# Asking for the next piece of the token mix's weights at the end of the following step

## The chip, the core and the metric

The kernel runs on one core of one Trainium2 chip. The metric is the device time in microseconds (us). Each time stated for a kernel is the median of its runs. One execution of the kernel before was also profiled: that execution has a time of its own, and every row shown below comes from it.

The engines are called PE (matrix multiply), DVE (vector), ACT (scalar), POOL (GpSimd) and SP. SP computes nothing here: it issues nearly all DMAs, one after the other, in the order in which the program was written. A DMA that has to wait for a buffer holds every DMA behind it in SP's queue.

## The reference, cut to what matters

Three blocks follow one another: attention with a computed bias, a token mix with a channel mix, and a routed expert layer. Only the first and the weights of the second matter here.

```python
scores = scale * np.matmul(q, k.transpose(0, 1, 3, 2))          # q, k, v: (2, 8, 576, 64)
h = np.maximum(x @ w1 + b1, 0.0)                                # per pair of positions, 32 hidden
bias = h @ w2                                                   # (576, 576, 8)
scores = scores + bias.transpose(2, 0, 1)[None, :, :, :]
attn = np.exp(scores - np.max(scores, axis=-1, keepdims=True))  # then divided by its row sum
x = np.matmul(attn, v)
...
h = np.maximum(xt @ w_tok1, 0.0) @ w_tok2                       # token mix, 576 -> 256 -> 576
```

The token mix's weights w_tok1 (576 x 256) and w_tok2 (256 x 576) arrive as 64-bit floats. They are read during attention in nine pieces, each decoded to 32 bits on the chip.

## The kernel before, in words

Attention is a list of 40 steps, written out by hand: `for s in range(N + 2)`. The 576 query rows are cut into five row blocks (`its`: the 64 rows that are left over first, then four blocks of 128), and each block takes eight steps, one for each pair of heads of each batch. Step s computes the scores of its pair on PE (L359), adds the bias and takes the row minimum of the negated sum on DVE (L337), takes the exponential on ACT (L340), and does the transposes and the product with V for the steps just before it.

Beside these, steps 8 to 31 compute the bias of the row block to come, one group of 16 rows a step. `bias_hidden` makes the hidden units `hd` (L487 on ACT, L490 on DVE and POOL). `bias_mm` multiplies them on PE (L500), ACT copies the product out of PSUM into a tile `ev` (L503), and a DMA (L511) moves `ev` into 16 partitions of the block's bias tile. There are two `ev` buffers, so the copy of a group waits until the DMA of the group two steps before has landed. Eight groups make one bias tile, and the first scores of a new row block (steps 16, 24, 32) need all eight.

Within a step the order of work comes from `ORDER`. In "bias" (most steps from 8 on) `late` stands before `bias_mm`. In "edge" (steps 15, 23 and 31, the last of a row block) `bias_mm` stands second, before that step's scores, while `query_rest` stands near the end, with `late` behind it. Each order is also the order of SP's queue. `query_rest` runs in odd steps and issues four DMAs `qt<-qs` (L328). `load_q` runs at the top of even steps and issues `qn<-in_q_dram` (L245).

`late_step(s)` runs what the table `LATE` has for step s, among it `decode(p)` of a piece p, in steps 10, 12, 14, 16, 17, 20, 22, 24 and 26. `decode_f64` is one operation on ACT (L724) and three on DVE (L726, L728, L730), from the 64-bit tile `raw64` into 32 bits. `raw64` has two buffers (tag "kn"). Pieces 0 and 1 are fetched in step 8; every later `fetch` (L704) stands right behind the `decode` that frees its buffer. Pieces 0 to 3 are 256 KB each. Piece 4 is two DMAs of 128 KB. Pieces 5 to 8 are 288 KB each.

In the text, bias(13) means the DMA `bias<-ev` of step 13, ev(15) means ACT's copy L503 in step 15, and fetch 4 means the DMA or DMAs of piece 4.

Of the kernel before, what the change touches and what calls it, by code (L numbers as in the profile page):

```python
# [98 lines left out]
def body(ctx, tc, q, k, v, w1, b1, w2, wt1, wt2, wc1, wc2, wg, wl, mw1, mw2,  # L99
# [17 lines left out]
    with tc.manual_schedule():  # L117
        tok = ctx.enter_context(ExitStack())
        mix = TokenMix(nc, x)
        attention(tc, nc, tok, mix, q, k, v, w1, b1, w2, c_L, c_id, ident, x, wt1, wt2, prefill)  # L120
        if "x" in dbg:
            nc.sync.dma_start(dbg["x"], x)
        R = Routing(tc, nc, wg, wl, ident, c_tok, c_small, x2d, meta)
        X = Experts(tc, nc, R, Rings(tc, ctx, "big", side="right"), x_p, mw1, mw2, ident, x2d, meta, out)
        mixer(tc, nc, tok, mix, wc1, wc2, ident, x, R, X)
        if "x2" in dbg:
            nc.sync.dma_start(dbg["x2"], x2d)
        X.rest()
        X.close()
        R.close()  # L130


def attention(tc, nc, tok, mix, q, k, v, w1, b1, w2, c_L, c_id, ident, x, wt1, wt2, prefill):
# [10 lines left out]
    with ExitStack() as ctx:  # L144
# [65 lines left out]
        def load_k(i):  # L210

            b, pr = divmod(i, NP)
            n = nat_p.tile([128, 20, D], F32, name="kn", tag="kn", bufs=2)
            main, hs = n[:, 0:16].rearrange("p (n h) d -> p n h d", h=4), k[b, 2 * pr:2 * pr + 4]
            for j in range(NIT):
                nc.sync.dma_start(main[:, j], hs[:, 128 * j:128 * j + 128].rearrange("h p d -> p h d"))
            nc.sync.dma_start(n[0:64, 16:20], hs[:, 512:S].rearrange("h p d -> p h d"))
            for j in range(2):
                nat["k", i + j] = main[:, :, 2 * j:2 * j + 2], n[0:64, 16 + 2 * j:18 + 2 * j]

        def load_v(b):
            n = kv_p.tile([128, NIT + 1, H, D], F32, name=f"v{b}")


            nv, src = n.rearrange("p n (a e) d -> e p n a d", e=2), v[b].rearrange("(a e) p d -> e p a d", e=2)
            for e in range(2):
                r, z = (slice(64 * o, 64 * o + 64) for o in (e, 1 - e))
                nc.gpsimd.memset(nv[e][z, NIT], 0.0)
                for j in range(NIT):
                    nc.sync.dma_start(nv[e][:, j], src[e][64 * e + 128 * j:64 * e + 128 * j + 128])  # L230
                nc.sync.dma_start(nv[e][r, NIT], src[e][0:64] if e else src[e][512:S])
            nat["v", b] = n

        def load_q(it, i):

            b, pr = divmod(i, NP)
            n = nat_p.tile([128, 4, D], F32, name="qn", tag="qn", bufs=2)
            if it == NIT:
                tv = q[b, :, 512:S].rearrange("(a e) p d -> e p a d", e=2)
                for e in range(2):  # L240
                    nc.sync.dma_start(n[64 * e:64 * e + 64], tv[e])
                for j in range(NP):
                    nat["q", it, i + j] = n[:, j]
            else:
                nc.sync.dma_start(n, q[b, 2 * pr:2 * pr + 4, 128 * it:128 * it + 128].rearrange("h p d -> p h d"))  # L245
                nat["q", it, i] = n
# [268 lines left out]
        pieces = [(0, n) for n in range(5)] + [(1, n, a) for n in range(2) for a in range(2)]  # L515
        wt1_s = None

        def fetch(p):
            n = p[1]
            if p[0] == 0:  # L520
                src = wt1[128 * n:min(128 * n + 128, S)]
            else:
                src = wt2[128 * n:128 * n + 128, HALF * p[2]:HALF * p[2] + HALF]
            raws[p] = fetch_f64(nc, nat_p, src, "kn", 2, p[0] == 0 and n == 4)
# [65 lines left out]
        late = {}  # L590
# [13 lines left out]
        def late_step(s):  # L604
            for f, *a in late.get(s, ()):
                f(*a)
                if f is decode and pieces:
                    fetch(pieces.pop(0))

        load_const()  # L610
        bias_setup()
# [16 lines left out]
        for s in range(N + 2):  # L628

            bias = gi < len(groups) and s < N and s >= B * NP * (its.index(groups[gi] // 8) - 1)  # L630
            at = lambda d, n=N: steps[s + d] if 0 <= s + d < n else None
            two = lambda d: (s + d) % 2 == 0 and s + d >= B * NP and at(d)
            hide = groups[gi + 1] if bias and gi + 1 < len(groups) else None
            todo = {
                "late": (late_step, (s,)), "mix": (mixes[s][0], mixes[s][1:]) if s in mixes else (None, None),
                "tail_split": (tail_split, at(2, B * NP)), "tail_T": (tail_T, at(1, B * NP)),
                "query_T": (query_T, two(QO[0])), "query_split": (query_split, two(QO[1])), "query_rest": (query_rest, two(QO[2])),
                "key_split": (key_split, at(2, B * NP)),
                "normalize": (normalize, at(0)), "last_T": (last_T, at(-1)),
                "values": (values, at(-2)), "out_T": (out_T, at(-2)),  # L640
                "bias_mm": (bias_mm, (groups[gi],) if bias else None),
            }
            for j in range(4):
                todo[f"hidden{j}"] = bias_hidden, hide is not None and (hide, (j,))
                todo[f"key_T{j}"] = key_T, j < 2 and at(2, B * NP) and (*at(2), j)
                todo[f"scores{j}"] = scores, at(0) and (*at(0), j)
                todo[f"prob_T{j}"] = prob_T, at(-1) and (*at(-1), j)
            if two(QO[3]):
                load_q(*steps[s + QO[3]])
            for name in ORDER["edge" if bias and s % (B * NP) == B * NP - 1 else "first" if s < 3 else "mixed" if s < B * NP else "bias" if bias else "plain"]:  # L650
                f, a = todo[name]
                if a:
                    f(*(a[1:] if f in (key_split, key_T) else a))
            gi += bias
            if s == 1:
                load_k(6)
            if s == 2:
                load_v(1)
            if s == 10:
                prefill()  # L660
            if s == 8:
                for _ in range(2):
                    fetch(pieces.pop(0))
# [31 lines left out]
def fetch_f64(nc, pool, src, tag, bufs, twice=False):  # L695

    p = src.shape[0]
    wide = src.dtype != F32
    raw = pool.tile([128, *src.shape[1:], *([2] if wide else [])], I32 if wide else F32, name="raw64", tag=tag, bufs=bufs)
    if wide:  # L700
        e = "p k (n t) -> p k n t" if len(src.shape) == 3 else "p (n t) -> p n t"
        src = src.bitcast(I32).rearrange(e, t=2)
    for j in range(1 + twice):
        nc.sync.dma_start(raw[p * j:p * j + p], src)  # L704
    return raw, wide
# [1053 lines left out]
```

## Time and profile before

| | us |
|---|---|
| median of 3 runs | 587.43 (586.86 to 589.52) |
| the profiled execution's own time | 590.45 |
| its span, first to last instruction | 588.6 |
| PE busy | 546.4 (93% of the span) |
| DVE busy | 382.6 (65%) |
| ACT busy | 329.9 (56%) |
| POOL busy | 242.0 (41%) |
| mean granted TensorE clock | 0.978 of full speed |

Times in the rows count from the span's start. In a timeline row the first number is the start, the second the duration in us, and a bracket at the end gives how long the engine had been idle just before and what it waited for. Attention takes about the first 230 us. Steps 10 to 23, in which the change acts, lie between about 80 and 160 us.

### The profile page before, as it was taken

How to read it: one execution, taken by the hardware profiler on the slowest of the kernel's cores; microseconds unless marked ns; L12 is line 12 of the kernel's file. 1: busy time of each engine (PE TensorE's matmuls, PEld its weight loads, DVE VectorE, ACT ScalarE, POOL GpSimd, SP SyncE). 2: the span in 40 equal slices, each digit the busy share in tenths (PEclk: the TensorE clock that was granted, in tenths of full speed). 3: DMA queues.
4: the chain of work that ended last, by engine and by line, in shares of the span. 5: the costliest groups of instructions: out<-in, count | busy, mean ns of one | idle time of the engine just before them, and what ended most of it. 6: DMA issues, size and time to landing. Idle time of an engine off the chain costs nothing.

```text
span 588.6 us, 11960 instructions
## 1 busy us (share of the span) xinstructions
PE 546.4 (93%) x4306; PEld 431.8 (73%) x4306; DVE 382.6 (65%) x896; ACT 329.9 (56%) x608; POOL 242.0 (41%) x230
## 2 busy tenths in 40 slices
PE   8689699799899999998999999999999999999992
PEld 3356477577677797778999877787777778787871
DVE  6699588498797675598988644724374134668650
ACT  5578589489699685244444324221322257777760
POOL 4567466347566163034444400310004234666541
PEclk9899899799999999999999999999999999999997
DMA  7997989699777461044454010062001985566950
GB/s 160 133 171 130 150 158 157 84 170 167 118 132 134 87 167 52 0 143 117 141 155 164 4 69 21 1 245 96 37 18 21 359 306 179 152 225 240 369 187 12
DMA packets 72110, 79.90 MB, mean 136 GB/s; under 512 B 36822, under 2 KB 51420, under 8 KB 72044
## 3 DMA queue, kind: packets, MB, share of 16 engines
q1 hardware_dynamic: 67276, 73.72, 52.0%
q0 software_dynamic: 2176, 5.26, 2.7%
q8 instruction: 36, 0.59, 0.5%
q10 hardware_dynamic: 2592, 0.09, 0.3%
q14 instruction: 30, 0.25, 0.2%
HBM read 72.08 MB, written 5.34 MB: 132 GB/s over the span
## 4 chain that ended last, share of the span: by engine, by line
PE 62%; DVE 11%; DMA 11%; ACT 6%; issue 5%; SPq 2%; POOL 2%; ACTq 0%; POOLq 0%; DVEq 0%
PE ph L744 19%; PE po L744 15%; DMA bias<-ev 9%; PE py L744 5%; PE tp L425 4%; PE ps L500 4%; PE ps L359 3%; PE tp L410 3%; ACT t L340 2%; DVE t L337 2%; DVE K L272 1%; PE tp L744 1%; PE tp L1444 1%; DMA mt<-meta 1%; DMA raw<-in_moe_w_ch_dram 1%
## 5 line engine op out<-in xcount | busy, mean ns | idle before, releaser
L490 POOL TENSOR_SCALAR hd<-tabs,sc,negb 128x576 f32<-128x576 f32 x32 | 76.0, 2377 | 3.4 <-DMA qt<-qs 1.8
L340 ACT ACTIVATE t<-t,st 128x576 f32<-128x576 f32 x72 | 55.4, 771 | 27.4 <-DVE st L337 27.2
L337 DVE CUSTOM_DVE_ANT_0 t<-ps,bias 128x576 f32<-128x576 f32 x72 | 52.4, 751 | 23.1 <-DMA bias<-ev 13.1
L744 PE MATMUL po<-cw,h 128*128 128x512 f32 x272 | 67.3, 395 | 0.0
L359 PE MATMUL ps<-K,qt 128*128 128x288 f32 x320 | 56.3, 316 | 8.8 <-ACT ev L503 5.1
L744 PEld LDWEIGHTS po<-cw,h 128*128 128x128 f32 x272 | 49.8, 188 | 10.0 <-issue 0.4
L1407 DVE TENSOR_TENSOR big<-raw,big 128x1024 fp32r<-128x1024 f32 x30 | 42.6, 1441 | 22.2 <-ACT big L1406 22.1
L359 PEld LDWEIGHTS ps<-K,qt 128*128 128x128 f32 x320 | 46.4, 197 | 11.3 <-ACT ev L503 5.6
L500 PE MATMUL ps<-hd,wblk 128*32 128x288 f32 x576 | 44.1, 419 | 8.7 <-DVE st L337 6.3
L425 PE MATMUL tp<-pt,v 128*64 128x128 f32 (+1 forms) x800 | 49.8, 271 | 0.5 <-DVE K L272 0.5
L744 PE MATMUL py<-big,hT 128*128 128x512 f32 x184 | 47.8, 400 | 0.4 <-POOL big L1407 0.4
L1185 POOL DMA_INDIRECT meta<-tokid,posi x10 | 10.0, 998 | 90.9 <-DVE tokid L1182 55.0
L425 PEld LDWEIGHTS tp<-pt,v 128*64 128x64 f32 x800 | 40.7, 139 | 7.9 <-issue 5.2
L1406 ACT CAST big<-raw 128x1024 fp32r<-128x1024 f32 x44 | 44.2, 1055 | 2.8 <-DMA big<-in_moe_w_dram 1.0
L744 PE MATMUL ph<-big,xT 128*128 128x512 f32 x168 | 42.9, 403 | 0.0
L490 DVE TENSOR_SCALAR hd<-tabs,sc,negb 128x576 f32<-128x576 f32 x69 | 41.3, 630 | 0.2
L744 PEld LDWEIGHTS py<-big,hT 128*128 128x128 f32 x184 | 33.8, 188 | 8.6 <-POOL big L1407 0.8
L736 POOL TENSOR_TENSOR big<-wf,big 128x512 fp32r<-128x512 f32 x12 | 18.8, 1564 | 50.2 <-ACT big L735 50.2
L487 ACT ACTIVATE hd<-tabs,b1c,sc 128x576 f32<-128x576 f32 x43 | 36.9, 865 | 3.8 <-DVE sc L458 3.7
L1407 POOL TENSOR_TENSOR big<-raw,big 128x1024 fp32r<-128x1024 f32 x10 | 27.8, 2776 | 25.1 <-ACT big L1406 25.1
L503 ACT ACTIVATE ev<-ps,cb 128x576 f32<-128x576 f32 x36 | 26.6, 739 | 19.1 <-DMA bias<-ev 10.1
L744 PEld LDWEIGHTS ph<-big,xT 128*128 128x128 f32 x168 | 30.6, 189 | 8.6 <-issue 1.6
(302 smaller groups left out, 1196.2 us busy)
## 6 DMA issues: line engine op xcount, KB each, us to landing
raw<-in_moe_w_dram SPq DMA_DIRECT2D x48, 512.0 KB
raw<-in_moe_w_ch_dram SPq DMA_DIRECT2D x24, 512.0 KB
bias<-ev SPq DMA_DIRECT2D x32, 288.0 KB
qt<-qs SPq DMA_DIRECT2D x64, 128.0 KB
lw<-in_moe_w_dram SPq DMA_DIRECT2D x16, 512.0 KB
big<-in_moe_w_dram SPq DMA_DIRECT2D x8, 512.0 KB
lw<-in_moe_w_dram SPq DMA_DIRECT2D x16, 256.0 KB
big<-in_moe_w_dram SPq DMA_DIRECT2D x16, 256.0 KB
```

Source lines behind the costliest of these rows:

```text
L337: nc.vector.tensor_tensor_reduce(t.rearrange("p (a j) -> p a j", a=2), ps[:, :, 0:HALF], bs.rearrange("p (a j) -> p a j", a=2), op0=ALU.ad ...
L340: nc.scalar.activation(t, t, AF.Exp, bias=st[:, j:j + 1], scale=-1.0, accum_out=st[:, 2 + j:3 + j])
L359: nc.tensor.matmul(ps[:, hf, 0:HALF], lhsT=qt[:, j], rhs=K[k][:, hf * HALF:(hf + 1) * HALF], start=j == pairs[0][0], stop=j == pairs[-1][0])
L425: nc.tensor.matmul(po[64 * h:64 * h + 64, 0:rhs.shape[1]], lhsT=lhsT, rhs=rhs, start=j == 0, stop=j == 4)
L487: nc.scalar.activation(hd[:, qq], Lt[:, o:o + S], AF.Relu, bias=b1c, scale=sc[:, c])
L490: eng.tensor_scalar(hd[:, qq], Lt[:, o:o + S], sc[:, c], negb, ALU.mult, ALU.max)
L500: nc.tensor.matmul(ps[32 * qq:32 * qq + 32, hf, 0:HALF], lhsT=wblk, rhs=hd[:, qq, hf * HALF:(hf + 1) * HALF], start=True, stop=True)
L503: nc.scalar.activation(ev.rearrange("p (a b) -> p a b", a=2), ps[:, :, 0:HALF], AF.Identity, bias=cbs[hidden_by(g).replace("P", "V")])
L736: nc.gpsimd.tensor_tensor(lo, src, hi.bitcast(F32), ALU.subtract)
L744: nc.tensor.matmul(out, lhsT=lhs[a], rhs=rhs[b], start=first and i == 0, stop=last and i == 2)
L1406: nc.scalar.copy(hi, raw)
L1407: (nc.gpsimd if c == 3 and t else nc.vector).tensor_tensor(lo, raw, hi.bitcast(F32), ALU.subtract)
```

## The change

The fetch no longer stands behind its `decode`. Instead a new function, called at the end of step s, issues one fetch if step s - 1 had a `decode`. The seven fetches that stood in steps 10, 12, 14, 16, 17, 20 and 22 now stand at the ends of steps 11, 13, 15, 17, 18, 21 and 23. The pieces, their order, the buffers and the decodes stay as they were.

```diff
         def late_step(s):
             for f, *a in late.get(s, ()):
                 f(*a)
-                if f is decode and pieces:
-                    fetch(pieces.pop(0))
+
+        def late_fetch(s):
+
+            if pieces and any(f is decode for f, *_ in late.get(s, ())):
+                fetch(pieces.pop(0))
 
         load_const()
         bias_setup()
@@ -652,6 +655,7 @@
                 if a:
                     f(*(a[1:] if f in (key_split, key_T) else a))
             gi += bias
+            late_fetch(s - 1)
             if s == 1:
                 load_k(6)
             if s == 2:
```

## Rows read from the trace of the kernel before

**Rows 1.** The page, part 2: busy share of the DMA engines in 40 slices of 14.7 us.
```profile
DMA  7997989699777461044454010062001985566950
```

**Rows 2.** Who waited for whom, 75 to 200 us: total, times, longest.
```profile
ACT ev L503 <- DMA bias<-ev: 5.7, 2, 5.0
...
DVE t L337 <- DMA bias<-ev: 3.8, 2, 2.0
```

**Rows 3.** The timeline of PE, steps 15, 23 and the start of 24.
```profile
104.86 0.77 PE L359 MATMUL ps<-K,qt 128*128 128x288 f32 x4
109.85 1.33 PE L359 MATMUL ps<-K,qt 128*128 128x288 f32 x4 [4.22 <-ACT ev L503]
...
149.23 1.18 PE L500 MATMUL ps<-hd,wblk 128*32 128x288 f32 x16
...
152.53 0.80 PE L359 MATMUL ps<-K,qt 128*128 128x288 f32 x4 [0.89 <-ACT ev L503]
...
159.56 0.69 PE L500 MATMUL ps<-hd,wblk 128*32 128x288 f32 x8 [1.66 <-DVE st L337]
```

**Rows 4.** The timeline of ACT: copies to ev (L503) and decodes (L724).
```profile
101.73 0.45 ACT L724 ACTIVATE wt_s<-raw 128x256 f32<-128x256 f32 x1
...
109.06 0.74 ACT L503 ACTIVATE ev<-ps,cb 128x576 f32<-128x576 f32 x1 [5.03 <-DMA bias<-ev]
...
123.92 0.43 ACT L724 ACTIVATE wt_s<-raw 128x256 f32<-128x256 f32 x1
...
151.73 0.74 ACT L503 ACTIVATE ev<-ps,cb 128x576 f32<-128x576 f32 x1 [2.24 <-PE ps L359]
...
192.25 0.74 ACT L503 ACTIVATE ev<-ps,cb 128x576 f32<-128x576 f32 x1 [1.04 <-PE ps L500]
```

**Rows 5.** The chain that ended last: start, us from issue to landing.
```profile
90.35 7.43 DMA bias<-ev
...
99.20 9.76 DMA bias<-ev
...
152.50 6.08 DMA bias<-ev
...
193.02 5.03 DMA bias<-ev
```

**Rows 6.** Stretches: length, five engines' busy us, PEclk, DMA share, GB/s.
```profile
85.00:110.00 25.00, 20.78 (x240) 15.49 (x239) 19.12 (x59) 17.74 (x36) 13.97 (x8) 0.99 1.04 147
...
96.00:97.00 1.00, 1.00 (x20) 0.59 (x20) 1.00 (x5) 1.00 (x3) 1.00 (x1) 1.00 1.00 277
...
122.00:123.00 1.00, 1.00 (x22) 0.83 (x22) 1.00 (x5) 1.00 (x2) 1.00 (x2) 1.00 0.79 286
...
156.00:157.00 1.00, 1.00 (x14) 0.81 (x14) 0.69 (x2) 1.00 (x2) 0.92 (x2) 1.00 0.43 45
```

**Rows 7.** The same view and columns, around the fall of PE's clock.
```profile
109.00:110.00 1.00, 0.15 (x1) 0.15 (x1) 0.00 (x0) 0.94 (x2) 0.00 (x0) 0.65 0.47 49
...
115.00:116.00 1.00, 1.00 (x6) 1.00 (x6) 0.29 (x1) 0.98 (x2) 0.91 (x2) 0.50 0.00 0
116.00:117.00 1.00, 1.00 (x10) 0.81 (x11) 0.81 (x3) 0.37 (x1) 1.00 (x2) 0.93 0.00 0
```

**Rows 8.** The timeline of SP: fetches (L704) and the qt DMAs of step 15.
```profile
94.07 0.33 SPq L704 DMA_DIRECT2D raw<-in_moe_w_tok_dram  x1
...
104.06 1.16 SPq L704 DMA_DIRECT2D raw<-in_moe_w_tok_dram  x2
...
116.08 2.67 SPq L328 DMA_DIRECT2D qt<-qs  x4
...
120.64 0.35 SPq L704 DMA_DIRECT2D raw<-in_moe_w_tok_dram  x1
...
150.19 0.35 SPq L704 DMA_DIRECT2D raw<-in_moe_w_tok_dram  x1
```

**Rows 9.** The timeline of DVE, first scores of row block two (step 16).
```profile
116.19 0.76 DVE L337 CUSTOM_DVE_ANT_0 t<-ps,bias 128x576 f32<-128x576 f32 x1 [0.67 <-PE ps L359]
```

## The prediction, made before the changed kernel was run

> **What bounds the kernel now.** I read the page's slices first, for the stretch in which the change acts. The DMA engines are nine tenths busy or close to it in most of the first ten slices [rows 1], which is attention up to 147 us. So the change moves traffic inside a stretch where the DMA engines have little left; elsewhere such a move would hardly show.
>
> Then the waits between 75 and 200 us, to see who suffers [rows 2]. Two kinds matter: ACT's copy to `ev` waits for a bias DMA to land (5.7 us in two waits, one of them 5.0), and the softmax on DVE waits for one (3.8 us in two).
>
> Then PE's own timeline, because only what PE loses reaches the end. From 85 to 110 us PE is busy 20.78 of 25 us [rows 6], and the 4.22 us left are one hole, in step 15 before 109.85 [rows 3]. Around step 23 there are two more, 0.89 us before 152.53 and 1.66 us before 159.56. These three, 6.77 us together, are all that this change can win back, with what PE loses to a half clock behind the first hole. That hole is worth following: PE waits for ev(15), which starts at 109.06 after 5.03 us of idle ACT [rows 4], and which waited for bias(13), issued at 99.20 and landed 9.76 us later [rows 5]. Bias DMAs took 7.43 us from 90.35, 6.08 from 152.50 and 5.03 from 193.02; the last is from step 31, where no fetch is near. So a bias DMA costs some 5 us at best, and the rest is traffic ahead of it or beside it.
>
> **The change, part by part.** It adds no instruction and no byte. Seven fetches move by one to two steps, past these entries of SP's queue: the bias DMA of the step of the decode, what the next step puts there (`load_q` if it is even, the four `qt` DMAs if it is odd), and that next step's bias DMA. None of the passed entries now stands behind a wait for the decode's last DVE operation. New waits: none on SP, since the buffer has long been free.
>
> Even-step bias DMAs are issued earlier. That alone is worth nothing: the two `ev` waits sum to 5.7 us, the long one is step 15's, so 0.6 us is all that ACT ever waited for one of them, and PE had no hole there [rows 2, 3]. The two `ev` buffers are the cover.
>
> *Term a, step 15.* Fetch 3, asked for at 94.07 [rows 8], stands ahead of bias(13); after, it stands behind. The DMA engines are continuously busy in that stretch (share 1.04 [rows 6]), so what leaves the queue ahead shortens the landing by its service time. A fetch shows as a burst: 277 GB/s in 96 to 97 us [rows 6]; 256 KB at that rate is 0.95 us. Fetch 2 is ahead of bias(13) before and after, fetch 4 behind in both. So bias(13) lands at about 108.0 instead of 108.96 and PE resumes at 108.9.
>
> The clock takes a part of it. PE stopped at 105.63; its granted clock fell from 2.4 to 1.2 GHz at 109.3 (mean 0.65 over 109 to 110) and came back at 116.07 (0.93 over 116 to 117) [rows 3, 7]. If it still falls there, the 0.95 us gained are 0.4 at full and 0.55 at half speed, worth **0.68 us**. Bounds: nothing, if a fetch behind a bias DMA slows it as much as one ahead; the whole hole of 4.22 us and half of the 6.22 us from 109.85 to 116.07, if the stall ends.
>
> *Term b, ev(23).* It starts at 151.73, and the row names PE's L359, but the copy reads nothing of that. Its own product, L500, ended at 150.41 (149.23 + 1.18). In step 31, without a fetch nearby, ev(31) is released by L500 itself [rows 3, 4]. So I read the extra 1.3 us as the landing of bias(21), two steps back, and fetch 7 moves from ahead of bias(21) to behind it: 0.95 us again. PE's hole there is 0.89 us, so **0.89 us**. Bounds: 0 and 0.89.
>
> *Term c, bias(23).* Fetch 8, issued at 150.19, goes from ahead of bias(22) and bias(23) to behind the `qt` DMAs of step 23 [rows 8]. Bias(23) should then land like bias(31): 5.03 us instead of 6.08, **1.05 us** off the hole of 1.66 [rows 3, 5]. Bounds: 0 and 1.66.
>
> *Term d, the piece that is now late.* Six of the seven pieces keep time to spare. The shortest of them is piece 2, asked for behind bias(11) at 91 us and read by ACT at 101.73, 10.7 us later [rows 4, 5], longer than the slowest bias landing. Piece 4 is different. Step 15 has `query_rest` near its end, so fetch 4 moves from 104.06 to behind the four `qt` DMAs, which end at 118.75, and its two DMAs take 1.16 us of issue; ACT reads it at 123.92 [rows 4, 8]. Second half issued at 119.35. A fetch asked for at 120.64 had its burst in 122 to 123 us [rows 6, 8], about 2.4 us from issue to the last byte. Landing follows the data by about 2.2 us (bias(23) faded at 156.4, share 0.43 over 156 to 157, and landed at 158.58 [rows 5, 6]). That makes 4.6 us and 123.95: just too late or just in time. I take **+0.2 us**, by the nearest row. Bounds: 0, since earlier data gain nothing, and 2.9 us, if it takes the 7.43 us of a loaded bias DMA [rows 5]. ACT runs in order, so a late piece holds ev(17) and the exponentials of step 18.
>
> The Trainium skill (Trainium Kernel Development and Optimization, Best Practices) tells to double-buffer and overlap DMA with compute, which speaks against asking later; here the piece's time in hand before 123.92 falls from 19.9 to 5.2 us [rows 4, 8], and by that rule term d would be at its upper bound, 2.9 us, and the sum +0.3 us.
>
> *Sum.* -0.68 - 0.89 - 1.05 + 0.2 = **-2.4 us**. Against the profiled execution's own 590.45 (span 588.6 and 1.85 around it) that is 588.0. That execution stands 3.0 us above the median of the runs, with the same holes, so I take the sum off the median: 587.43 - 2.4 = **585.0 us**, 0.41% faster. Behind step 24 the rest follows attention's end and shifts as a whole, I assume.
>
> **The rivals.**
>
> *R1, the half clock goes too.* If PE resumes earlier or the fall comes at another moment, PE's work from 109.85 to 116.07 runs at full speed. Worth at most 3.1 us, but the first softmax of step 16, at 116.19 [rows 9], needs bias(15), issued when ev(15) ends (109.8) and landing no sooner than 5.03 us later, 114.8; so 1.35 us. Total -0.95 - 1.35 - 0.89 - 1.05 + 0.2 = -4.0: 583.4 us. For it: 3.3 us of idleness remain instead of 4.22. Against it: the clock fell 3.7 us after PE stopped, not far above what remains [rows 3, 7]. Chance 0.15.
>
> *R2, a fetch behind costs what it cost ahead.* Bias(13) took 4.7 us more than bias(31), far more than one burst of 0.95. If the DMAs behind share the engines with it, fetch 3, now right behind, slows it as before, and fetch 7 does so to bias(21): terms a and b are gone, c and d stay, -0.85: 586.6 us. Chance 0.22. The Trainium skill (DMA: Bandwidth & Descriptors, Queues, rings and completion order) says that one engine starts descriptors in order, but a later one may finish its write first; that permits this rival and does not price it. No row before shows which holds.
>
> *R3, slower.* Fetch 4 lands late. Its place is the decode in step 17, on ACT at 123.92. With the loaded 7.43 us it is 2.9 us late; ACT stops, DVE's L728 and PE follow, and a hole like step 15's would cost half a clock again, 3.1 us [rows 3, 7]. 2.9 + 3.1 - 2.6 (terms a to c) = +3.4: 590.8 us. Without the clock it turns slower than before once the piece is 2.6 us late. Against it: the DMA engines moved nothing from 115 to 117 us [rows 7], so the queue is short there. Chance 0.08.
>
> *R4, it does nothing that shows.* The fetches certainly move, as SP's queue is in order, but the bias DMAs may be bound by their own writes into 16 partitions: 587.4 us. Chance 0.10. The forecast keeps 0.45.
>
> **How the numbers follow.** About 0.5% (2.9 us) is what a measurement of this kernel can tell from no change. Faster by more than that: nearly all of R1 (0.14) and a third of the forecast's case, where a or c come out larger (0.16): 0.30. Slower by more: R3 and a little scatter: 0.08. The rest 0.62. The range goes from 582.2, below R1 by the scatter of the runs shown, to 588.5, above R4 by the same; R3 and a complete end of the stall lie outside.
>
> **What would show it.** In the changed trace: fetches right behind bias(11), bias(13) and bias(21), and behind the `qt` DMAs of steps 15 and 23; bias(13) landing in about 8.8 us, ACT's wait before ev(15) near 4.1 us and PE's hole near 3.3, with a half clock after it; ev(23) released by L500; bias(23) landing in 5.0 us and the 1.66 us hole down to 0.6; less than 0.5 us of idle ACT before step 17's L724. It is wrong if the landing of bias(13) does not change (R2), if no half clock follows step 15 (R1), or if ACT waits for piece 4 by more than 2 us (R3).

## The result, and the profile after

The changed kernel takes 584.0 us (median of 20 runs, 581.57 to 587.8) against 588.91 us for the kernel before (20 runs, 586.36 to 592.03). The ratio is 0.991, with a 95% interval of 0.9891 to 0.9929: 0.9% faster. The forecast was 0.41%.

The page of the changed kernel: the span and PE's busy time, then the granted clock and the DMA engines' busy share in 40 slices.

```profile
span 582.3 us, 11959 instructions
## 1 busy us (share of the span) xinstructions
PE 545.5 (94%) x4306; PEld 430.3 (74%) x4306; DVE 383.9 (66%) x896; ACT 329.5 (57%) x608; POOL 242.1 (42%) x230
...
PEclk8979889999999999999999999999999999999997
DMA  6997988698697351143443020081002985566950
```

PE's busy time hardly moved (545.5 us against 546.4); idle time went. Of the waits between 75 and 200 us [rows 2], ACT's for a bias DMA is gone from the list, and DVE's fell from 3.8 to 1.8 us:

```profile
ACT ev L503 <- PE ps L500: 4.8, 7, 1.0
...
DVE t L337 <- DMA bias<-ev: 1.8, 1, 1.8
```

PE's timeline, every idle stretch that it lists from 75 to 160 us. The holes of 4.22, 0.89 and 1.66 us [rows 3], and one of 0.33 not shown there, became four that sum to 2.67 us:

```profile
112.25 1.18 PE L500 MATMUL ps<-hd,wblk 128*32 128x288 f32 x16 [0.64 <-DVE st L337]
122.75 1.18 PE L500 MATMUL ps<-hd,wblk 128*32 128x288 f32 x16 [0.48 <-DVE st L337]
152.64 1.18 PE L500 MATMUL ps<-hd,wblk 128*32 128x288 f32 x16 [1.09 <-DVE st L337]
156.69 0.33 PE L397 MATMUL tp<-ident,t 128*128 128x128 f32 x1 [0.46 <-DVE x L448]
```

The stretches of [rows 6] (length, busy us of PE, PEld, DVE, ACT and POOL, granted clock, DMA share, GB/s). PE is busy throughout 85 to 110 us, and no half clock follows; before, the clock fell to 0.5 there [rows 7]:

```profile
85.00:110.00 25.00, 25.00 (x286) 19.60 (x284) 21.90 (x67) 22.32 (x46) 14.68 (x9) 1.00 0.85 154
110.00:117.00 7.00, 6.36 (x73) 4.87 (x74) 5.82 (x18) 5.15 (x11) 3.71 (x3) 1.00 0.56 137
```

ACT's timeline, with ev(15), the decode of piece 4 and ev(23), the counterparts of [rows 4]. Both copies to `ev` are released by their own product L500; the decode has no idle time before it:

```profile
105.39 0.74 ACT L503 ACTIVATE ev<-ps,cb 128x576 f32<-128x576 f32 x1 [1.04 <-PE ps L500]
...
118.76 0.42 ACT L728 ACTIVATE wt_s<-raw 128x256 f32<-128x256 f32 x1
...
145.33 0.74 ACT L503 ACTIVATE ev<-ps,cb 128x576 f32<-128x576 f32 x1 [1.04 <-PE ps L500]
```

SP's timeline around step 15, the counterpart of [rows 8]:

```profile
99.51 0.58 SPq L511 DMA_DIRECT2D bias<-ev  x1
100.19 0.54 SPq L708 DMA_DIRECT2D raw<-in_moe_w_tok_dram  x1
100.78 0.43 SPq L245 DMA_DIRECT2D qn<-in_q_dram  x1
103.86 2.84 SPq L511 DMA_DIRECT2D bias<-ev  x2
110.84 2.63 SPq L328 DMA_DIRECT2D qt<-qs  x4
113.57 1.20 SPq L708 DMA_DIRECT2D raw<-in_moe_w_tok_dram  x2
```

Bias(13), issued at 99.51, had landed when ev(15) started at 105.39: at most 5.9 us instead of 9.76 [rows 5]. Bias(14) goes out at 103.86, right when ev(14) ends (103.10 + 0.74); before, it waited behind fetch 4 until 105.3.

### The profile page after: what moved, and what is told of

Its sections match the earlier page's. It is cut to its first block, busy times and chain, and to the rows that moved or that the text cites. A ratio compares the mean times of both kernels' runs of the same rounds, so it can differ in the third digit from the quotient of the medians.

```text
span 582.3 us, 11959 instructions
## 1 busy us (share of the span) xinstructions
PE 545.5 (94%) x4306; PEld 430.3 (74%) x4306; DVE 383.9 (66%) x896; ACT 329.5 (57%) x608; POOL 242.1 (42%) x230
## 4 chain that ended last, share of the span: by engine, by line
PE 65%; DVE 12%; DMA 7%; issue 5%; ACT 5%; SPq 2%; POOL 2%; ACTq 0%; POOLq 0%; DVEq 0%
PE ph L748 20%; PE po L748 16%; DMA bias<-ev 6%; PE py L748 5%; PE ps L500 5%; PE tp L425 4%; PE ps L359 3%; PE tp L410 3%; DVE t L337 2%; ACT t L340 2%; PE tp L748 1%; DVE K L272 1%; DMA mt<-meta 1%; PE tp L1448 1%; DVE raw L732 1%
## 5 line engine op out<-in xcount | busy, mean ns | idle before, releaser
L359 PE MATMUL ps<-K,qt 128*128 128x288 f32 x320 | 54.0, 309 | 4.4 <-DVE qt L199 3.5
L500 PE MATMUL ps<-hd,wblk 128*32 128x288 f32 x576 | 47.7, 440 | 7.5 <-DVE st L337 6.5
L359 PEld LDWEIGHTS ps<-K,qt 128*128 128x128 f32 x320 | 45.0, 192 | 6.7 <-DVE qt L199 2.3
L500 PEld LDWEIGHTS ps<-hd,wblk 128*32 128x32 f32 x576 | 17.2, 115 | 24.1 <-DVE st L337 7.9
```

The source lines that it names most:

```text
L359: nc.tensor.matmul(ps[:, hf, 0:HALF], lhsT=qt[:, j], rhs=K[k][:, hf * HALF:(hf + 1) * HALF], start=j == pairs[0][0], stop=j == pairs[-1][0])
L500: nc.tensor.matmul(ps[32 * qq:32 * qq + 32, hf, 0:HALF], lhsT=wblk, rhs=hd[:, qq, hf * HALF:(hf + 1) * HALF], start=True, stop=True)
```

## The experiments

Two theories after this: the *hold* (SP stood at the fetch until the decode's last DVE operation, and the even-step bias DMA behind it went out late) and the *traffic* (the fetch's bytes lay ahead of the bias DMAs). Ratios are to the kernel before, run beside each.

**third_buffer.** Fetch in its old place in the program, but no wait:

```diff
-            raws[p] = fetch_f64(nc, nat_p, src, "kn", 2, p[0] == 0 and n == 4)
+            i = order.index(p)
+            tag, bufs = ("raw3", 1) if i % 3 == 2 else ("kn", 2)
+            raws[p] = fetch_f64(nc, nat_p, src, tag, bufs, p[0] == 0 and n == 4)
```

> The kernel before, with a third buffer for the pieces: each fetch stays where it was, ahead of the bias DMA of the decode's step, but no longer waits for the decode, so it holds nothing. Theory H (the hold: what cost the time was SP standing at the fetch until the decode's last DVE operation, which issued the even-step bias DMAs 1.0 to 1.8 us late): the gain of the changed kernel is there, 0.7 to 1.0% under the kernel before, and PE's hole before ev(15) is under 1 us. Theory T (the traffic: 256 KB ahead of each pair of bias DMAs): as the kernel before within 0.2%, hole about 4.2 us and the half clock behind it.

583.77 us, ratio 0.9925 (0.9898 to 0.9953): nearly the whole gain, by the hold theory. Its SP and ACT timelines:

```profile
99.89 0.58 SPq L511 DMA_DIRECT2D bias<-ev  x1
100.52 0.59 SPq L245 DMA_DIRECT2D qn<-in_q_dram  x1
101.20 1.18 SPq L707 DMA_DIRECT2D raw<-in_moe_w_tok_dram  x2
104.26 2.88 SPq L511 DMA_DIRECT2D bias<-ev  x2
```
```profile
105.78 0.74 ACT L503 ACTIVATE ev<-ps,cb 128x576 f32<-128x576 f32 x1 [1.04 <-PE ps L500]
```

The order in the queue is that of the kernel before: fetch 4, then bias(14) and bias(15). But SP, which waits for nothing, asks for the fetch at 101.20, 3 us before bias(14) at 104.26; in the kernel before these were 104.06 and 105.32, 1.3 us apart. So the order alone does not make the cost; when the issues come matters too.

**hold_only** and **no_hold.** The changed kernel with a 1 KB DMA in the seven old places; in the first it reads the decode's result, in the control the identity matrix:

```diff
+        scratch = scr_p.tile([16, 16], F32, name="scratch")
...
                 f(*a)
+                if f is decode and s < 24:
+                    p = a[0]
+                    done = raws[p] if p[0] else wt1_s[:, p[1]]
+                    nc.sync.dma_start(scratch[0:16], done[0:16, 0:16])
```

> The changed kernel, with a 1 KB DMA in each of the seven old places that reads the decode's result, so SP waits there for the decode as before, while the fetch and its bytes stay in the new place. Adds seven issues of about 0.4 us. H: the time of the kernel before within 0.3%, hole of 3 to 5 us before ev(15). T: the time of the changed kernel, 0.7 to 1.0% under the kernel before.

> The control of the run with the added wait: the same seven 1 KB DMAs in the same places, reading the identity matrix, which is there from the start, so SP waits for nothing. Both theories: the time of the changed kernel within 0.2%, no hole before ev(15). If it is slower, the added issues cost by themselves and the other run must be read against this one.

With the hold 586.11 us, 0.996 (0.994 to 0.9979); the control 584.27 us, 0.9919 (0.9893 to 0.9945). So the waits cost 1.84 us (586.11 - 584.27, medians of 12 and 6 runs), with no byte of a fetch moved. That is less than half of what the hold theory alone had asked for, and more than the traffic theory had. SP's timeline with the hold, step 14; ACT's at ev(15) with the hold; PE's at step 16 with the hold; and PE's at the same place in the control:

```profile
105.57 0.33 SPq L612 DMA_DIRECT2D scratch<-wt_s  x1
106.00 2.24 SPq L512 DMA_DIRECT2D bias<-ev  x2
```
```profile
106.50 0.74 ACT L504 ACTIVATE ev<-ps,cb 128x576 f32<-128x576 f32 x1 [1.48 <-DMA bias<-ev]
```
```profile
114.35 1.18 PE L501 MATMUL ps<-hd,wblk 128*32 128x288 f32 x16 [1.68 <-DVE st L338]
```
```profile
113.72 1.18 PE L501 MATMUL ps<-hd,wblk 128*32 128x288 f32 x16 [0.79 <-DVE st L338]
```

With the hold ev(15) waits 1.48 us for bias(13), which stands behind a held bias(12); in the control ev(15) is released by its own product. The hold also puts bias(14) 1.3 us before bias(15) instead of 2.3 (issued at 106.00 and 107.27 here, at 105.19 and 107.48 in the control), and the first scores of the next row block wait for both.

**same_step.** The fetch at the end of the decode's own step: no hold, but its bytes ahead of the next step's `qt` and bias DMAs.

```diff
-            late_fetch(s - 1)
+            late_fetch(s)
```

> The fetch at the end of the step of its decode: behind that step's bias DMA, but still ahead of the next step's qt DMAs and of the odd-step bias DMA that ev(15), ev(23) and the next row block wait for. H: all of the gain, 0.7 to 1.0%, since no bias DMA stands behind the wait. T: little of it, under 0.3%, hole before ev(15) of 3 us or more, since bias(13) and bias(23) still have the bytes ahead.

585.99 us, 0.9961 (0.9938 to 0.9984): less than half the gain, and 1.72 us above the control no_hold, so bytes in this place count too. Bias(13) took 6.71 us (the chain that ended last), and ACT waited for it:

```profile
99.12 6.71 DMA bias<-ev
```
```profile
105.93 0.74 ACT L503 ACTIVATE ev<-ps,cb 128x576 f32<-128x576 f32 x1 [1.95 <-DMA bias<-ev]
```

**behind_qt.** One place earlier than the change: behind the `qt` DMAs, straight ahead of the odd-step bias DMA.

```diff
+                if name == "query_rest":
+                    late_fetch(s - 1)
             gi += bias
-            late_fetch(s - 1)
```

> The changed kernel with each fetch one place earlier: behind the qt DMAs and ahead of the odd-step bias DMA. SP waits for nothing there. If only the hold costs, as the changed kernel within 0.2% and no wait of ev(15). If the bytes straight ahead of bias(13) count too, that DMA lands 1 to 2 us later, ev(15) waits 0.5 to 2 us for it, and the time is 0.2 to 0.4% above the changed kernel.

584.36 us, 0.9938 (0.9907 to 0.997). The interval doesn't tell it from the change. The profiled execution, at 585.91 us, has the mechanism: ACT waited for bias(13), which took 7.57 us.

```profile
108.20 0.74 ACT L503 ACTIVATE ev<-ps,cb 128x576 f32<-128x576 f32 x1 [3.90 <-DMA bias<-ev]
```

**first_three** and **last_four.** The change for the decodes of steps 10 to 14 alone, or of steps 16 to 22 alone (the other fetches stay behind their `decode`). The diff is that of first_three; last_four has `s < 15` and `s > 15` in the two places:

```diff
+                if f is decode and pieces and s > 15:
+                    fetch(pieces.pop(0))
...
-            if pieces and any(f is decode for f, *_ in late.get(s, ())):
+            if pieces and s < 15 and any(f is decode for f, *_ in late.get(s, ())):
```

> Only the fetches of steps 10, 12 and 14 are moved; those of steps 16 to 22 stand where they stood before. If the gain is mostly the stall of step 15 (4.2 us of hole and up to 3.1 us of half clock), this has most of it: 0.6 to 0.8% under the kernel before. If steps 15 and 23 count alike, as the prediction's terms had it (0.7 against 1.9 us), about a quarter: 0.1 to 0.3%.

> Only the fetches of steps 16, 17, 20 and 22 are moved. First case: the stall of step 15 is there as before, 0.1 to 0.3% under the kernel before, hole before the first scores of step 24 about 1 us smaller. By the prediction's terms b and c: 0.3% (1.9 us).

585.92 us, 0.996 (0.9937 to 0.9984), and 586.64 us, 0.997 (0.9949 to 0.9991): 2.4 and 1.7 us off 588.33. They add up to 4.1 of the 4.9 us. In first_three step 15 has no stall, but another came, in step 19, behind the unmoved fetches of steps 16 and 17: the chain's bias DMA, then ACT's wait.

```profile
120.98 10.78 DMA bias<-ev
```
```profile
131.87 0.74 ACT L503 ACTIVATE ev<-ps,cb 128x576 f32<-128x576 f32 x1 [3.50 <-DMA bias<-ev]
```

In last_four, whose program up to step 15 is that of the kernel before, ACT's timeline has a shorter wait for bias(13) than the 5.03 us of [rows 4], and no half clock followed. PE's timeline has the larger hole one step later, before step 16's L500:

```profile
105.82 0.74 ACT L503 ACTIVATE ev<-ps,cb 128x576 f32<-128x576 f32 x1 [2.03 <-DMA bias<-ev]
```
```profile
106.61 0.80 PE L359 MATMUL ps<-K,qt 128*128 128x288 f32 x4 [0.68 <-ACT ev L503]
...
114.38 1.18 PE L500 MATMUL ps<-hd,wblk 128*32 128x288 f32 x16 [2.39 <-DVE st L337]
```

The changed kernel has only 0.64 us of these 3.07. So the stall's size and place vary between executions; the profiled one before, 1.5 us above the median of 20, had a large one.

**hold_edges** and **hold_others.** The 1 KB DMA that waits, in steps 14 and 22 only, or in the five other steps only (`if f is decode and s in (14, 22)`, `s in (10, 12, 16, 17, 20)`).

> The changed kernel with the 1 KB DMA that waits for the decode in steps 14 and 22 only, the even steps just before the edge steps 15 and 23. Theory E (the hold costs at the edges: it issues bias(14) and bias(22) so late that bias(15) and bias(23), which the next row block waits for, land behind them): nearly all of the cost of the seven holds is here, 585.5 to 586.5 us, 0.35 to 0.45% under the kernel before. Theory S (each hold adds to the backlog in the queue): a third of that cost or less, under 585.0 us, at least 0.6% under.

> The changed kernel with the 1 KB DMA that waits for the decode in steps 10, 12, 16, 17 and 20 only. E: as without any hold, 583.8 to 584.8 us, 0.6 to 0.9% under the kernel before. S: two thirds of the cost or more, 585.3 us or above, at most 0.5% under.

587.64 us, 0.997 (0.9952 to 0.9989), and 585.81 us, 0.9936 (0.9915 to 0.9957). Neither theory fits. In the ratios the two edge steps cost 0.6% over the change's 0.991, clear of its interval, and more than theory E had asked for. The other five cost 0.26%, which the intervals don't tell from nothing; nor do they tell whether the two costs add up to that of the seven in hold_only (0.5%). The profiled executions show late DMAs in both. With holds at the edges alone bias(15) took 6.38 us; with the others alone bias(13) was late, as in hold_only:

```profile
105.89 6.38 DMA bias<-ev
```
```profile
106.13 0.74 ACT L504 ACTIVATE ev<-ps,cb 128x576 f32<-128x576 f32 x1 [1.48 <-DMA bias<-ev]
```

**twice.** A second 256 KB into an unread tile behind each moved fetch:

```diff
-                fetch(pieces.pop(0))
+                p = pieces.pop(0)
+                fetch(p)
+                fetch_f64(nc, nat_p, wt1[128 * (s % 4):128 * (s % 4) + 128], "spare", 1)
```

> The changed kernel with a second fetch of 256 KB, into a tile that nothing reads, behind each moved fetch: 1.8 MB more in the same stretch, all in the new places. Leaves nothing out. If the new place is one that nothing waits behind, within 0.2% of the changed kernel. If the DMA engines have no room left in the stretch (the share is 0.82 to 0.85 of 85 to 110 us without it), the stall before ev(15) is back and the time is 0.5% or more above the changed kernel.

588.46 us, 0.9987 (0.9965 to 1.001): the whole gain is gone. So the stretch has no room for 1.8 MB more, even in the new places. But ev(15) did not wait for a DMA; the largest hole came one step later, at the first scores of step 16 (PE's timeline), with a half clock behind it. What the softmax there waited for, the trace does not name. The stretch moved 169 GB/s at a share of 0.93, more than the kernel before at 1.04.

```profile
115.42 1.18 PE L500 MATMUL ps<-hd,wblk 128*32 128x288 f32 x16 [2.05 <-DVE st L337]
```
```profile
85.00:110.00 25.00, 25.00 (x295) 19.05 (x283) 22.30 (x68) 22.32 (x46) 14.02 (x8) 1.00 0.93 169
```

**dma_alone.** The computation is left out. Only the DMAs of a step pair run, in 14 groups; each group is issued, then DVE reads each landing (the inner loop, cut):

```python
for group in ("b", "t", "f", "n", "bb", "bt", "bn", "fb", "ft", "tb", "btbn", "fbtbn", "btbfn", "bftbn"):
    for _ in range(3):
        for r in [what[w]() for w in group]:
            r()
        ...
```

> Leaves the whole computation out and writes zeros: only the DMAs of one step pair, issued from SP in 14 groups, three times each, with DVE reading each landing. Measures bias (b), the four qt (t), a 256 KB fetch (f) and qn (n), alone and one behind the other: b, t, f, n, bb, bt, bn, fb, ft, tb, btbn, fbtbn, btbfn, bftbn. If the engines simply serve in order, a group takes the sum of its members' data times: fbtbn is 1 us longer than btbn, and the second b lands 1 us later. If transfers that overlap slow each other, b behind or beside t takes more than its time alone, and a fetch ahead of btbn costs the second b more than 1 us, one behind it nothing.

A letter is one DMA: b a bias DMA, t a `qt` DMA, f a fetch, n a `qn` DMA. One repeat each of btbn, fbtbn, btbfn and bftbn, first SP's issue of the group's first DMA, then DVE's read of its second bias DMA:

```profile
188.57 0.59 SPq L122 DMA_DIRECT2D bias<-ev  x1
...
210.75 0.35 SPq L132 DMA_DIRECT2D raw<-in_moe_w_tok_dram  x1
...
245.21 0.60 SPq L122 DMA_DIRECT2D bias<-ev  x1
...
278.03 0.59 SPq L122 DMA_DIRECT2D bias<-ev  x1
```
```profile
198.09 0.14 DVE L123 COPY seen<-bias 16x1 f32<-16x1 f32 x1 [3.48 <-DMA bias<-ev]
...
221.86 0.14 DVE L123 COPY seen<-bias 16x1 f32<-16x1 f32 x1 [3.85 <-DMA bias<-ev]
...
254.68 0.14 DVE L123 COPY seen<-bias 16x1 f32<-16x1 f32 x1 [3.43 <-DMA bias<-ev]
...
288.24 0.14 DVE L123 COPY seen<-bias 16x1 f32<-16x1 f32 x1 [3.54 <-DMA bias<-ev]
```

From first issue to the read: 9.52 us without a fetch, 11.11 with one ahead, 9.47 with one behind the second bias DMA, 10.21 with one behind the first. The other repeats with one ahead gave 11.30 and 10.48. These times hold SP's own work for the extra issue, 0.4 us when the fetch goes first (210.75 to 211.15) and 0.7 between. Counted from its own issue, the first bias DMA is read after 5.4 to 5.95 us with a fetch ahead, against 4.9 without: 0.5 to 1.1 us for the bytes. With a fetch between, the second bias DMA is read 6.2 us after its own issue, as without a fetch. So with nothing else running, bytes ahead cost a bias DMA about what term a assumed, and bytes behind nothing.

**spread.** An attempt to beat both: later decodes, so that most fetches leave the crowded stretch.

```diff
-... decode=[10, 12, 14, 16, 17, 20, 22, 24, 26], split_wt2=[-3, -4, 0, -4, 8, 21, 23, 25, 28], ...
+... decode=[10, 16, 18, 22, 25, 27, 29, 31, 33], split_wt2=[-3, -4, 0, -4, 8, 28, 30, 32, 34], ...
```

> The changed kernel with the decodes of pieces 1 to 8 later (steps 16, 18, 22, 25, 27, 29, 31, 33 instead of 12, 14, 16, 17, 20, 22, 24, 26), so that the moved fetches stand at the ends of steps 11, 17, 19, 23, 26, 28 and 30: four of the seven leave or almost leave the stretch in which the DMA engines are short. If bytes in that stretch still cost the changed kernel something, PE's holes after steps 15 and 23 (0.64 and 1.09 us there) shrink to the 0.6 us of step 31 and the time is 0.1 to 0.3% under the changed kernel, 0.992 to 0.988 of the kernel before. If it has no such cost left, the same within 0.1%. If the decodes and splits, now beside steps 28 to 34, hold ACT and DVE there, it is slower than the changed kernel.

589.88 us, 1.0018 (0.9998 to 1.0038). PE's timeline at step 24 shows the gain, 0.23 us where the change has 1.09. The profiled execution, the fastest of 12, lost more around step 30, where PE waits for hidden units on POOL, which now had a split of the weights beside them:

```profile
150.55 1.18 PE L500 MATMUL ps<-hd,wblk 128*32 128x288 f32 x16 [0.23 <-DVE st L337]
...
184.77 2.14 PE L500 MATMUL ps<-hd,wblk 128*32 128x288 f32 x14 [2.24 <-POOL hd L490]
```

## Why the prediction was right, and where it was not

The direction and the place were right: the stall behind the bias DMAs in steps 15 and 23. 584.0 us lies inside the range, but the gain is about twice the forecast, and the likeliest case (within 0.5%) did not come. That the range held is partly luck: its lower end was set for R1, whose reason turned out to be another.

**The step that failed** is "Even-step bias DMAs are issued earlier. That alone is worth nothing". The cover named for it, the two `ev` buffers, guards ACT against one late landing. It does not keep the late issue from crowding the odd-step bias DMA behind it, which ACT and the next row block do wait for. hold_only against no_hold measured the hold at 1.84 us without any byte of a fetch. There bias(12) left 1.0 us after ev(12) was done, ev(15) waited 1.48 us for bias(13), and PE's hole before the L500 of step 16 was 1.68 us instead of 0.79. third_buffer, which keeps the order of the queue and removes the wait, had 0.9925. The Trainium skill (DMA: Bandwidth & Descriptors, Anatomy of one DMA) says that DMA engines do not wait on semaphores: a wait happens on the issuing sequencer, before dispatch. The trace agrees: bias(14) left at 103.86, when ev(14) was done; before, it left at 105.32, 1.8 us after its ev(14) (102.81 + 0.74). I had read the wait and priced only who waited for the held DMA itself.

**Term a** was mis-sized with it: -0.68 us forecast, with term d +0.2, against 2.4 us measured in first_three. One fetch's service alone is about what was assumed (0.5 to 1.1 us in dma_alone against 0.95). The two causes each cost about half: the hold 1.84 us, and the bytes ahead of the odd-step bias DMA 1.72 (same_step 585.99 - no_hold 584.27), together 3.56 of the 4.05 us between no_hold and the kernel before beside it (588.32). But in third_buffer a fetch ahead of both bias DMAs, asked for 3 us earlier, cost nothing that shows. My reading is that the wait costs twice: it holds the even-step bias DMA, and it moves the fetch's bytes to just ahead of the odd-step one. It fits these four runs, but no run moved the fetch's time alone. The wait of ev(15) does not add up in this way: 1.48 us with the hold alone, 1.95 with the bytes alone, and with both 2.03 in last_four and 5.03 in the profiled execution before.

**Terms b and c** held: -1.94 us forecast, 1.7 us measured in last_four (0.5 to 3.0 by its interval). Ev(23) is released by L500, as predicted; PE's hole before step 24's L500 is 1.09 us, not the 0.6 foreseen.

**Term d** was nothing: fetch 4's second half was issued at about 114.2 and read at 118.76 without idle time, so it landed within 4.6 us, the estimate itself.

**R1** named the right sign: no half clock follows step 15, and its 583.4 us is nearer than the forecast. Its reason was another, though; the clock did not fall at a better moment, the hole that let it fall was gone. **R2** falls: with fetch 3 right behind it (issued at 99.51 and 100.19) bias(13) landed in at most 5.9 us, and in dma_alone a fetch behind the second bias DMA cost it nothing. **R3** did not occur here, **R4** neither.

What stays open: how a bias DMA comes to 9.76 or 10.78 us in the full kernel, when no group in dma_alone brought the first one above 6 us from its issue; why its size varies between executions of one program (last_four), and whether the costs of single holds add up. The traffic of the compute engines beside it was not tried.

## What to carry to other kernels

A DMA that waits for its buffer in an in-order queue must be priced by everything it holds back, down to the transfer that somebody does wait for. Either more buffers or a later place removes that wait. Where the DMA engines are nearly full, ask also how many bytes stand ahead of that transfer, and put weights that are needed late behind it.

## What the runs showed of the hardware

- The DMA engines delivered more while less busy: 147 GB/s at a share of 1.04 over 85 to 110 us before, 154 GB/s at 0.85 after. In twice they delivered 169 GB/s at 0.93, so more bytes alone do not raise the engine time per byte; what raised it before, no run tells.
- In dma_alone a bias DMA (288 KB into 16 partitions), with nothing else running, is read 4.5 to 4.9 us after its issue, and a second one behind it 2.3 us later, some 130 GB/s; a fetch (256 KB into 128 partitions) is read in under 3 us.
